# Cosine attention and a cosine-gated MLP on one core: quad 5's softmax sums inverted through DRAM instead of spread by TensorE

## The chip, the cores and the metric

One Trainium2 chip, one of its cores. The metric is the time of one execution on the device in microseconds (us); the kernel before has a median of 417.52 us in three runs (416.75 to 418.28).

## What is computed

The reference is attention with normalised queries and keys, followed by a two-layer network whose activation is h cos(h):

```python
q_n = q / (norm(q, axis=-1) + 1e-06)            # q, k, v: 8 batches x 12 heads x 448 x 64
k_n = k / (norm(k, axis=-1) + 1e-06)
attn = softmax(q_n @ k_n.T / tau)               # tau = 0.1
x = (attn @ v), heads side by side              # 3584 tokens x 768
h = x @ w_in                                    # 768 x 2048
out = (h * cos(h)) @ w_out                      # 2048 x 768
```

## The kernel before, in words

**Quads and blocks.** Four heads of one batch make a *quad*; a batch has 3 quads, so there are 24, and quad n belongs to block n // 3 (a block is one batch of 448 tokens). For each quad the squares of its queries and keys are formed (L491, on POOL), summed (L495, DVE), turned into inverse norms (L521 and L524 on ACT, L527 and L530 on DVE), and the scaled copies Qn and Kn are made (L542, POOL). A transposing DMA (L585, issued by SP) turns them into qT and kT; quads 3 and 4 are transposed on TensorE (L564).

**Scores.** A quad has 7 score steps. A step is four 64x64 matmuls (L601) into a pair of PSUM banks, and one exp on ACT (L608) that writes the bf16 tile E. Three bank pairs take turns. When the 7 steps are done, an AV product of 28 matmuls (`gather`, L637) sums E with V, and DVE copies it to AVs (L644).

**Dividing by the sums.** The softmax is divided late. For a *round* of one or two quads, `sums` (its matmuls are L724) adds E over the keys by a matmul with a 0/1 matrix, with 32-column tiles, so that a row of sums stands in 16 equal partitions. ACT takes the log and the exp of its negative (L733, L734), which is the inverse. This has to be multiplied to AVs, where a sum's value is needed in 64 partitions. So SP writes the rows to a DRAM scratch `rscr` (L737) and reads them back, each row into 64 partitions, into the tile R (L743, two reads for a quad, 224 KB each); then POOL multiplies AVs by R into xT (L748, one instruction for both column blocks of a quad). There are two R tiles: quad n uses R[n % 2]. The rounds are [3, 4], [5], [6, 7], [8, 9] and so on; quads 0 to 2 are done otherwise.

**Quad 5 alone** is treated differently in the kernel before. It is the last quad of block 1 and its inverse is needed first of all by the second W1 stage. Its inverse is written to a corner of gT (`Zg`) that is still free, two matmuls in float32 with a selecting matrix `selB` spread it over the partitions in PSUM (`spread_out`, L759; each is two instructions in the trace), and DVE multiplies AVs with that bank (L761), a column block at a time. `selB` is made by an iota on POOL (L395) and a compare on DVE (L397) at the start.

**The MLP.** Block c's W1 stage is 96 matmuls (L774, 128x448), in 8 pairs of 6-step sums over xT's six column blocks (two for each quad). Each pair goes through ACT, DVE, ACT, DVE (L792, L793, L795, L798) into gT. The first `early` pairs of a stage are started with the blocks 0 to 3 only, as one instruction group that waits for all four, and are completed later with blocks 4 and 5: for block 0 two pairs, for the others one. Between the W1 stages, the W2 matmuls of the block (L833, 128x384, 16 to a sum) are dealt out between the scores of coming quads; DVE copies their sums to osb (L851) and SP stores them (L857).

**What sets the order.** The program is first written as a list of operations with an engine, a reading and a writing set; each engine then works strictly in order. For the head and for the stage from the first W1 to the second (operations 0 to 538), the order on all engines is written out by hand as permutations (HEAD and STAGE). From there on TensorE keeps the program's order and a planner orders ACT, DVE, POOL and SP by a cost and due time of each operation; LEADS moves the due time of some of them. Waits between engines follow from what each operation reads and writes.

The spread's call, which the change removes, is this, in `sums`:

```python
if alone:
    return [lambda bk, a=a: spread_out(quads[0], a, bk) for a in range(2)]
```

Of the kernel before, what the change touches and what calls it, by code (L numbers as in the profile page):

```python
# [8 lines left out]
ALU = mybir.AluOpType  # L9
AX = mybir.AxisListType  # L10
F32 = mybir.dt.float32
BF16 = mybir.dt.bfloat16
I32 = mybir.dt.int32
# [7 lines left out]
class Planner:  # L21
# [60 lines left out]
    def flow(self, until):  # L82
# [25 lines left out]
        (1198, 8, -18.7),  # L108
        (555, 8, -10.5),
        (829, 20, -0.8),  # L110
# [194 lines left out]
def bass_cosine_attention__then__act_gcu_kernel(  # L305
# [9 lines left out]
    B, NH, S, D = q.shape  # L315
# [46 lines left out]
    selB = gT.ap().bitcast(F32)[:, NNB - 2:, S // 2:S // 2 + 128]  # L362
    Zg = gT.ap().bitcast(F32)[0:64, NNB - 4:NNB - 2, S // 2:]
    in_g = [("g", 1, NNB - i) for i in range(1, 5)]
# [6 lines left out]
    def bank(i, n=S, p0=0, p1=128):  # L371
        return PS.ap()[p0:p1, 512 * i:512 * i + n]
# [11 lines left out]
    def fill_sel(e):  # L384
# [9 lines left out]

    op("pool", 0.5, lambda e: e.iota(selB.bitcast(I32), [[-16, 2], [-32, 2], [0, 64]], base=0, channel_multiplier=1),  # L395
       w=["selB"] + in_g)
    op("dve", 0.3, lambda e: e.tensor_scalar(selB, selB.bitcast(I32), 0, None, ALU.is_equal), r=["selB"],  # L397
       w=["selB"] + in_g)
# [29 lines left out]
    def whole(bk):  # L428
        return cut("B", bk, ALL[0])
# [281 lines left out]
    def sums(quads, bk):  # L711
# [3 lines left out]
        alone = quads == [2 * QB - 1]  # L715
        z = int(alone)
# [13 lines left out]
        zz, src, at = Zs[0].ap()[0:32 * np_, :], bank(bk, S, 0, 32 * np_), [("Zs", z)]  # L730
        if alone:
            zz, src, at = Zg, src.rearrange("p (c f) -> p c f", c=2), at + in_g
        act("exp", 0.43, lambda e: e.activation(zz, src, ACT.Ln, bias=0.0, scale=1.0), r=whole(bk), w=at, lead=LEAD)  # L733
        act("exp", 0.45, lambda e: e.activation(zz, zz, ACT.Exp, bias=0.0, scale=-1.0), r=at, w=at, lead=LEAD)  # L734
        if alone:
            return [lambda bk, a=a: spread_out(quads[0], a, bk) for a in range(2)]
        op("sp", 0.6, lambda e: e.dma_start(rscr.ap()[8 * n:8 * n + rows, :], Zs[0].ap()[0:32 * np_:16, :]),  # L737
           r=[("Zs", z)], w=[("rs", n)], dma=("rs", z), moves=0.05, lead=LEAD)
        for i, qd in enumerate(quads):
# [7 lines left out]
            def product(qd=qd, u=u, sl=sl, b=b, c0=c0):  # L747
                op("pool", 2.04, lambda e: e.tensor_tensor(  # L748
                    xT[b % 2].ap()[:, c0:c0 + 2, :], AVs[sl].ap(), R[u].ap(), ALU.mult),
                    r=[("AV", sl), ("R", u, 0), ("R", u, 1)], w=[("x", b % 2, c0), ("x", b % 2, c0 + 1)], lead=LEAD)  # L750
# [5 lines left out]

    def spread_out(qd, a, bk):
        sl, b, c0 = qd % NA, qd // QB, 2 * (qd % QB)
        op("pe", 0.95, lambda e: e.matmul(bank(bk), selB[0:64, a, :], Zg, start=True, stop=True),  # L759
           r=[("Zs", 1), "selB", *in_g], w=whole(bk), mode="b")  # L760
        op("dve", 0.57, lambda e: e.tensor_tensor(xT[b % 2].ap()[:, c0 + a, :], AVs[sl].ap()[:, a, :], bank(bk), ALU.mult),  # L761
           r=[("AV", sl)] + whole(bk), w=[("x", b % 2, c0 + a)], lead=LEAD)
# [154 lines left out]
    def warm(n, bk=0):  # L917
# [35 lines left out]
    )  # L953
    HEAD = (
# [307 lines left out]
```

## Time and profile before

| | |
|---|---|
| median of three runs | 417.52 us (416.75 to 418.28) |
| the profiled execution, its own time | 417.49 us |
| its span, first to last instruction | 415.7 us |
| TensorE clock granted | 1.0 throughout |
| second W1 stage begins (chain) | 89.08 us |

The page's times are microseconds from the span's start. PE is TensorE, DVE VectorE, ACT ScalarE, POOL GpSimd, SP the engine that only issues DMAs. "Chain that ended last" is the sequence of pieces, followed back from the last instruction, each of which released the next. In the lists, "out<-in" are the kernel's tile names, and a bracket behind a row gives the idle time ahead of it and what ended it. Matmuls overlap and their ends are modelled, so a group's length is best read from the starts in the chain. Between the profiled execution's time and its span lie 1.8 us.

### The profile page before, as it was taken

The page shows a single profiled execution, that of the slowest core. Times are in us where ns is not written, and L with a number is a line of the kernel's source. Part 1 is how long each engine was busy: PE and PEld are TensorE (multiplying, and loading weights), DVE is VectorE, ACT ScalarE, POOL GpSimd, SP SyncE. Part 2 cuts the span into 40 slices and gives each one's busy share as a digit, 9 for nine tenths or more (in the row PEclk, how much of TensorE's full clock was granted, in tenths as well). Part 3 has the DMA queues.
Part 4 walks back from the last instruction along what each step waited for, and adds up shares of the span by engine and source line. Part 5 has one row for each costly group of instructions (what it writes and reads, how often), then busy time and mean ns, then how long its engine had stood idle before and what let it go on. Part 6 is the DMA issues. An engine that isn't in the chain of part 4 may idle for free.

```text
span 415.7 us, 8622 instructions
## 1 busy us (share of the span) xinstructions
PE 408.1 (98%) x3629; PEld 216.6 (52%) x3629; DVE 265.2 (64%) x359; ACT 304.8 (73%) x422; POOL 209.4 (50%) x145
## 2 busy tenths in 40 slices
PE   7999999999999999999999999999999999999996
PEld 6455545445554545545554555554554555555565
DVE  5887986567956559655985539845882328736931
ACT  5999899978988678886886757987797656605700
POOL 2666957898299971787429852477403214000000
PEclk9999999999999999999999999999999999999999
DMA  8999997957999996299518993099203423031023
GB/s 267 255 249 205 270 204 150 205 140 134 256 259 240 215 220 169 61 215 255 140 30 167 186 328 89 21 226 170 80 2 82 131 75 91 1 77 38 2 74 78
DMA packets 67224, 62.97 MB, mean 151 GB/s; under 512 B 36385, under 2 KB 59633, under 8 KB 67185
## 3 DMA queue, kind: packets, MB, share of 16 engines
q1 hardware_dynamic: 54816, 50.57, 48.2%
q0 software_dynamic: 12288, 11.80, 18.7%
q8 instruction: 28, 0.46, 0.5%
q14 instruction: 12, 0.09, 0.1%
q10 hardware_dynamic: 80, 0.05, 0.0%
HBM read 54.79 MB, written 11.15 MB: 159 GB/s over the span
## 4 chain that ended last, share of the span: by engine, by line
PE 91%; ACT 4%; DVE 3%; DMA 1%; issue 0%; SPq 0%; ACTq 0%
PE PS L774 35%; PE PS L833 34%; PE PS L601 8%; PE PS L637 7%; PE PS L724 4%; ACT E L608 2%; DMA Kf<-in_k_dram 1%; PE PS L667 1%; PE PS L810 1%; PE PS L618 1%; DVE Qn L542 1%; PE PS L564 1%; DVE n L495 0%; PE PS L759 0%; ACT ar L795 0%; ACT ar L792 0%
## 5 line engine op out<-in xcount | busy, mean ns | idle before, releaser
L608 ACT ACTIVATE E<-PS 128x896 bf16<-128x896 f32 x168 | 143.8, 922 | 19.4 <-PE PS L601 18.0
L833 PE MATMUL PS<-W,gT 128*128 128x384 bf16 x880 | 153.4, 327 | 0.0
L774 PE MATMUL PS<-xT,W 128*128 128x448 bf16 x768 | 147.8, 353 | 0.1
L833 PEld LDWEIGHTS PS<-W,gT 128*128 128x128 bf16 x880 | 81.8, 98 | 68.5 <-issue 14.8
L774 PEld LDWEIGHTS PS<-xT,W 128*128 128x128 bf16 x768 | 74.3, 98 | 71.0 <-issue 1.5
L792 ACT ACTIVATE ar<-PS 128x896 int32<-128x896 f32 (+1 forms) x72 | 59.0, 829 | 47.7 <-PE PS L774 47.1
L793 DVE SCALAR_TENSOR_TENSOR ar<-ar,PS 128x896 f32<-128x896 int32 (+1 forms) x72 | 69.3, 979 | 32.8 <-ACT ar L792 32.7
L748 POOL TENSOR_TENSOR xT<-AVs,R 128x896 bf16<-128x896 f32 x20 | 41.6, 2089 | 61.3 <-DMA R<-rscr 61.3
L798 DVE TENSOR_TENSOR gT<-PS,ar 128x896 bf16<-128x896 f32 (+1 forms) x72 | 69.3, 983 | 3.1 <-ACT ar L795 2.8
L795 ACT ACTIVATE ar<-ar 128x896 f32<-128x896 f32 (+1 forms) x72 | 60.7, 861 | 7.7 <-DVE ar L793 6.9
L851 DVE COPY osb<-PS 128x384 f32<-128x384 f32 x54 | 30.0, 556 | 53.7 <-PE PS L833 53.0
L542 POOL TENSOR_TENSOR Qn<-Qf,rr 128x896 bf16<-128x896 f32 x21 | 35.4, 1686 | 38.4 <-DVE rr L530 38.2
L601 PE MATMUL PS<-qT,kT 64*64 64x448 bf16 x672 | 49.0, 359 | 1.8 <-DVE kT L575 0.8
L644 DVE COPY AVs<-PS 128x896 f32<-128x896 f32 x21 | 22.9, 1090 | 31.3 <-PE PS L637 31.3
L491 POOL TENSOR_TENSOR sqk<-Kf 128x896 bf16<-128x896 f32 x21 | 35.3, 1680 | 13.3 <-DMA Kf<-in_k_dram 7.2
L491 POOL TENSOR_TENSOR sqq<-Qf 128x896 bf16<-128x896 f32 x21 | 35.3, 1682 | 8.9 <-DVE n L495 4.6
L542 POOL TENSOR_TENSOR Kn<-Kf,rr 128x896 bf16<-128x896 f32 (+1 forms) x22 | 36.6, 1668 | 0.0
L637 PE MATMUL PS<-E,Vb 64*64 64x448 bf16 x588 | 31.4, 349 | 0.0
L601 PEld LDWEIGHTS PS<-qT,kT 64*64 64x64 bf16 x672 | 15.3, 105 | 27.0 <-issue 9.8
L495 DVE TENSOR_REDUCE n<-sqk 128x14 f32<-128x896 bf16 (+2 forms) x24 | 24.9, 1039 | 3.6 <-POOL sqk L491 2.9
L495 DVE TENSOR_REDUCE n<-sqq 128x14 f32<-128x896 bf16 (+2 forms) x24 | 24.8, 1037 | 2.2 <-POOL sqq L491 2.1
L451 POOL DMA_DIRECT2D Vb<-in_v_dram x24 | 18.0, 750 | 16.4 <-PE PS L601 9.7
(68 smaller groups left out, 200.8 us busy)
## 6 DMA issues: line engine op xcount, KB each, us to landing
Qf<-in_q_dram SPq DMA_DIRECT2D x24, 448.0 KB, 5.0
out_dram<-osb SPq DMA_DIRECT2D x54, 192.0 KB, 3.0
Kf<-in_k_dram SPq DMA_DIRECT2D x23, 448.0 KB, 5.9
R<-rscr SPq DMA_DIRECT2D x40, 224.0 KB, 4.4
Vb<-in_v_dram POOLq DMA_DIRECT2D x24, 224.0 KB, 7.9
W<-in_moe_w_in_dram POOLq DMA_DIRECT2D x4, 768.0 KB, 11.3
W<-in_moe_w_out_dram POOLq DMA_DIRECT2D x4, 768.0 KB, 11.7
Kf<-in_k_dram SPq DMA_DIRECT2D x1, 320.0 KB, 4.7
```

The lines of the kernel that those rows point to most:

```text
L491: op(eng, (1.64 if eng == "pool" else 1.05) * n, lambda e: e.tensor_tensor(dst, src, src, ALU.mult), r=cut(nm + "f", s, part), w=at, after ...
L495: return op("dve", 0.05 + 0.94 * n, lambda e: e.tensor_reduce(out=n2[u].ap()[:, H * w:H * w + H] if part == ALL[0] else jr(n2[u], w, part) ...
L542: lambda e: e.tensor_tensor(n[u].ap()[:, j0:j1].rearrange("p j r d -> p r j d"), f[s].ap()[:, :, j0:j1], rb, ALU.mult),
L601: ins = e.matmul(bank(bs + r, S, 64 * a, 64 * a + 64), kT[u].ap()[64 * r:64 * r + 64, j, a, :], qT[u].ap()[64 * r:64 * r + 64, :, a, :], s ...
L608: act("exp", 0.806, lambda e: e.activation(E[es].ap(), two(bs), ACT.Exp, bias=0.0, scale=INV_TAU), r=pair(bs), w=[("E", es)], chain="E")
L637: ins = e.matmul(bank(bs + a, S, 64 * r, 64 * r + 64), Vb[vs].ap()[64 * a:64 * a + 64, r, j, :], E[es[j]].ap()[64 * a:64 * a + 64, r, :], ...
L774: ins = e.matmul(bank(bk + i2), W1.ap()[:, i, 128 * nb:128 * nb + 128], xT[c % 2].ap()[:, i, :], start=(i == 0), stop=(i == NKC - 1))
L792: op("act", 0.055 + 0.375 * n, lambda e: e.activation(ai, src, ACT.Identity, bias=0.25, scale=INV2PI), r=bs, w=at)
L793: op("dve", 0.06 + 0.47 * n, lambda e: e.scalar_tensor_tensor(a, ai, -2.0 * math.pi, src, ALU.mult, ALU.add), r=bs + at, w=at)
L795: act("sin", 0.09 + 0.375 * n, lambda e: e.activation(a, a, ACT.Sin, bias=GUARD * math.pi / 2.0, scale=GUARD), r=at, w=at)
L798: op("dve", 0.07 + 0.47 * n, lambda e: e.tensor_tensor(gT.ap()[:, f0:f1, col:col + S], src, a, ALU.mult), r=bs + at, w=[("g", c % 2, f) fo ...
L833: ins = e.matmul(bank(bk, HW), gT.ap()[:, f, col:col + 128], W2.ap()[:, f, HW * h:HW * h + HW], start=(f == 0), stop=(f == NNB - 1))
```

## The change

Quad 5's round goes the way of the other rounds: its inverse is written to DRAM and read back into R[1]. Its multiplication by AVs is done by DVE in two instructions, one for each column block, where the other quads have one on POOL. The two spreading products, their two DVE multiplications, `selB`, `Zg` and the two operations that made `selB` are gone. Block 1's W1 stage now starts two pairs early, as block 0's, instead of one. HEAD is the same order with the two removed operations left out; STAGE is another order; LEADS has one entry instead of three.

```diff
     LEADS = (
-        (1198, 8, -18.7),
-        (555, 8, -10.5),
-        (829, 20, -0.8),
+        (844, 1, -0.4),
     )
...
-    op("pool", 0.5, lambda e: e.iota(selB.bitcast(I32), [[-16, 2], [-32, 2], [0, 64]], base=0, channel_multiplier=1),
-       w=["selB"] + in_g)
-    op("dve", 0.3, lambda e: e.tensor_scalar(selB, selB.bitcast(I32), 0, None, ALU.is_equal), r=["selB"],
-       w=["selB"] + in_g)
...
-        zz, src, at = Zs[0].ap()[0:32 * np_, :], bank(bk, S, 0, 32 * np_), [("Zs", z)]
-        if alone:
-            zz, src, at = Zg, src.rearrange("p (c f) -> p c f", c=2), at + in_g
+        zz, src, at = Zs[0].ap()[0:32 * np_, :], bank(bk, S, 0, 32 * np_), ["Zs"]
...
-        if alone:
-            return [lambda bk, a=a: spread_out(quads[0], a, bk) for a in range(2)]
...
             def product(qd=qd, u=u, sl=sl, b=b, c0=c0):
+                if qd == 2 * QB - 1:
+                    for a in range(2):
+                        op("dve", 0.54, lambda e, a=a: e.tensor_tensor(
+                            xT[b % 2].ap()[:, c0 + a, :], AVs[sl].ap()[:, a], R[u].ap()[:, a], ALU.mult),
+                            r=[("AV", sl), ("R", u, 0), ("R", u, 1)], w=[("x", b % 2, c0 + a)], lead=LEAD)
+                    return
...
-    def spread_out(qd, a, bk):
-        sl, b, c0 = qd % NA, qd // QB, 2 * (qd % QB)
-        op("pe", 0.95, lambda e: e.matmul(bank(bk), selB[0:64, a, :], Zg, start=True, stop=True),
-           r=[("Zs", 1), "selB", *in_g], w=whole(bk), mode="b")
-        op("dve", 0.57, lambda e: e.tensor_tensor(xT[b % 2].ap()[:, c0 + a, :], AVs[sl].ap()[:, a, :], bank(bk), ALU.mult),
-           r=[("AV", sl)] + whole(bk), w=[("x", b % 2, c0 + a)], lead=LEAD)
...
-        late, early = 2 * (QB - 1), 1 if c else 2
+        late, early = 2 * (QB - 1), 1 if c > 1 else 2
```

STAGE's numbers say little to a reader, so here are the two orders resolved into instructions where they differ around the change.

PE, from the AV product of quad 3 (63.85 in the trace before) to the second W1 stage. V is an AV product, S a score step (S2: two of them), Mn a run of n W2 matmuls, T a transpose of seven 128x128 blocks, Z the sums of a round, P a spreading product; a bar is a change between groups of different tile shape (T and M have the same).

```
before  V S | M2 T T | S2 | M7 | S3 | Z(3,4) | V S2 | M6 | S2 | M8 | S2 V S | Z(5) | S3 | M14
        | S3 | M6 | P | S2 V S | P | S2 | M5, W1
after   V S | M4 T | S | T | S | M4 | S2 | Z(3,4) | S V S | M1 | S | M4 | S2 | M6 | S | M1
        | S V S2 | Z(5) | S3 | M14 | S2 | M9 | S2 V S | M5 | S2 | W1
```

SP, from the load of quad 9's query on (Q and K are loads of a query or key tile into the slot named, qT and kT transposing DMAs, "write" and "read" those of the scratch):

```
before  Q[0], K[0], qT(7), write(3,4), kT(7), read x2 R[1], read x2 R[0], Q[1], K[1], qT(8), kT(8), Q[2], stores ...
after   Q[0], write(3,4), K[0], qT(7), Q[1], kT(7), read x2 R[1], read x2 R[0], write(5), K[1], qT(8), kT(8),
        read x2 R[1] for quad 5, store, store, store, Q[2], stores ...
```

POOL, from quad 7's query scaling on:

```
before  Qn(7), square K, Kn(7), square Q, square K, square Q, product(3), product(4), square Q, Qn(8), square K, ...
after   Qn(7), square K, Kn(7), square Q, square K, Qn(8), Kn(8), product(3), product(4), square Q, square K, V load, ...
```

DVE, the last operations of the stage: before, AVs copy of quad 6, norm steps and the second multiplication of quad 5, norm steps, an osb copy, two norm sums (L495); after, AVs copy, a norm step, two osb copies, a norm step, a norm sum, the two multiplications of quad 5, a norm sum. On ACT the logs and exps (L733, L734) of rounds [3, 4] and [5] stand closer together than before: one score's exp lies between the two of [3, 4] (before four), none between the two of [5] (before three).

More of the change, by code (lines that the diff above doesn't have):

```diff
@@ L361, in bass_cosine_attention__then__act_gcu_kernel @@
     ident = sb("ident", [128, 128], BF16)
-    selB = gT.ap().bitcast(F32)[:, NNB - 2:, S // 2:S // 2 + 128]
-    Zg = gT.ap().bitcast(F32)[0:64, NNB - 4:NNB - 2, S // 2:]
-    in_g = [("g", 1, NNB - i) for i in range(1, 5)]
     sel = sb("sel", [128, 32], BF16)
@@ L714, in sums @@
         summed.update(quads)
-        alone = quads == [2 * QB - 1]
-        z = int(alone)
         np_ = 2 * len(quads)
@@ L729, in sums @@
            mode="s")
-        zz, src, at = Zs[0].ap()[0:32 * np_, :], bank(bk, S, 0, 32 * np_), [("Zs", z)]
-        if alone:
-            zz, src, at = Zg, src.rearrange("p (c f) -> p c f", c=2), at + in_g
+        zz, src, at = Zs[0].ap()[0:32 * np_, :], bank(bk, S, 0, 32 * np_), ["Zs"]
         act("exp", 0.43, lambda e: e.activation(zz, src, ACT.Ln, bias=0.0, scale=1.0), r=whole(bk), w=at, lead=LEAD)
         act("exp", 0.45, lambda e: e.activation(zz, zz, ACT.Exp, bias=0.0, scale=-1.0), r=at, w=at, lead=LEAD)
-        if alone:
-            return [lambda bk, a=a: spread_out(quads[0], a, bk) for a in range(2)]
         op("sp", 0.6, lambda e: e.dma_start(rscr.ap()[8 * n:8 * n + rows, :], Zs[0].ap()[0:32 * np_:16, :]),
-           r=[("Zs", z)], w=[("rs", n)], dma=("rs", z), moves=0.05, lead=LEAD)
+           r=["Zs"], w=[("rs", n)], dma=("rs", 0), moves=0.05, lead=LEAD)
         for i, qd in enumerate(quads):
```

56 rows, old and new, of tables (HEAD, STAGE) are left out of this document.

## The prediction

> **What bounds the kernel now.** I read the page first: its line of engines and the chain that ended last.
>
> ```profile
> span 415.7 us, 8622 instructions
> PE 408.1 (98%) x3629; PEld 216.6 (52%) x3629; DVE 265.2 (64%) x359; ACT 304.8 (73%) x422; POOL 209.4 (50%) x145
> PE 91%; ACT 4%; DVE 3%; DMA 1%; issue 0%; SPq 0%; ACTq 0%
> ```
>
> TensorE is the bound nearly everywhere: a microsecond that leaves its queue is gained, and one in which it waits is lost. Then the busy time by stretches, around the place of the change (columns: stretch, its length, busy us and instructions of PE, PEld, DVE, ACT, POOL, then clock, DMA share, GB/s).
>
> ```profile
> 77.00:78.00 1.00, 1.00 (x20) 0.44 (x14) 0.67 (x1) 1.00 (x2) 1.00 (x1) 1.00 0.51 113
> 79.00:80.00 1.00, 1.00 (x15) 0.43 (x8) 0.42 (x1) 1.00 (x2) 1.00 (x2) 1.00 0.05 5
> 81.00:82.00 1.00, 1.00 (x10) 0.49 (x12) 0.49 (x1) 1.00 (x3) 0.47 (x1) 1.00 0.91 262
> ```
>
> PE is full there at full clock (1.00 behind POOL's column), ACT nearly, and the DMA has holes at 77 to 80. Last, the chain in order of time (start, us, what):
>
> ```profile
> 58.50 0.94 ACT E L608
> ...
> 63.85 1.42 PE PS L637 x28
> ...
> 77.47 1.43 PE PS L724 x14
> 78.90 0.69 PE PS L601 x12
> 79.59 2.38 PE PS L833 x14
> ...
> 83.75 0.95 PE PS L759 x2
> 84.69 0.50 PE PS L601 x8
> 85.20 1.32 PE PS L637 x28
> 86.71 0.95 PE PS L759 x2
> 87.66 0.50 PE PS L601 x8
> 88.16 0.92 PE PS L833 x5
> 89.08 2.27 PE PS L774 x12
> ...
> 339.74 18.16 PE PS L774 x96
> 357.90 15.60 PE PS L833 x96
> ```
>
> Until 63.85 an exp (L608) still appears on the chain; from there to the second W1 stage (L774, from 89.08) every piece is PE's. One W1 matmul costs 18.16/96 = 0.189, one W2 matmul 15.60/96 = 0.1625. The chain also prices a change between groups of unlike tile shape: eight L601 matmuls take 0.50 and twelve 0.69, so four cost 0.19 and 0.12 is fixed; fourteen W2 matmuls take 2.38 for 14 x 0.1625 = 2.28, fixed 0.10. I use 0.115 for a **switch**.
>
> **PE's part of the change.** The two spreading products (L759) go: 0.95 each with the switch into it, 1.90 together. But the new written order cuts PE's work into smaller groups. By the two resolved lists shown with the diff, from quad 3's AV product (63.85) to the second W1 stage, the old one has 20 switches, 2 of them inside the two 0.95; the new one has 25. That adds (25 - 18) x 0.115 = 0.80. Scores, AV products, sums, transposes and W2 matmuls are the same in number. So PE could start W1 1.90 - 0.80 = 1.10 earlier, at 87.98. Ahead of 63.85 the new list has four more switches too (15 for 11); there an exp sets the pace, so I take 0, with 0.46 as the upper bound and 0.3 of gain as the lower, since one score is issued earlier.
>
> Another engine limits that start. W1's early parts wait for all four blocks of quads 3 and 4 at once, and POOL writes them (L748).
>
> ```profile
> 74.86 1.69 POOL L542 TENSOR_TENSOR Kn<-Kf,rr 128x896 bf16<-128x896 f32 x1
> 76.51 1.68 POOL L491 TENSOR_TENSOR sqq<-Qf 128x896 bf16<-128x896 f32 x1
> 78.15 1.68 POOL L491 TENSOR_TENSOR sqk<-Kf 128x896 bf16<-128x896 f32 x1
> 79.79 1.68 POOL L491 TENSOR_TENSOR sqq<-Qf 128x896 bf16<-128x896 f32 x1
> 83.77 4.12 POOL L748 TENSOR_TENSOR xT<-AVs,R 128x896 bf16<-128x896 f32 x2 [2.30 <-DMA R<-rscr]
> 87.85 1.68 POOL L491 TENSOR_TENSOR sqq<-Qf 128x896 bf16<-128x896 f32 x1
> ```
>
> POOL now idles 2.30 for R. The new list puts four operations of about 1.65 between the key scaling that ends at 76.55 and the products, where three stood: free at 76.55 + 4 x 1.65 = 83.15, still ahead of R. So the products stay at 83.77 and end at 83.77 + 4.12 = 87.89. PE and POOL thus both allow W1 at 88.0, no earlier, and **1.1 us is the most the change can give**.
>
> **Quad 5's inverse by the DRAM trip.** What was PE work becomes a chain through SP, the DMA, POOL's release of a buffer and DVE. SP's issues, before:
>
> ```profile
> 76.91 1.24 SPq L585 DMA_TRANSPOSE kT<-Kn  x1
> 78.19 3.53 SPq L743 DMA_DIRECT2D R<-rscr  x4
> ...
> 94.01 0.61 SPq L737 DMA_DIRECT2D rscr<-Zs  x1
> ...
> 325.16 2.51 SPq L743 DMA_DIRECT2D R<-rscr  x4
> ```
>
> The sum of quad 5 (L724) ends in the new order one stretch ahead of W1: three scores 0.69, fourteen W2 2.38, two scores 0.50, nine W2 9 x 0.1625 + 0.115 = 1.58, three scores with an AV product 86.71 - 84.69 = 2.02, five W2 0.92, two scores 0.50, a switch 0.115: 8.7 before 88.0, at 79.3. In the next round the sum ends at 92.78 (rows below) and SP issues the write at 94.01, 1.2 later.
>
> ```profile
> 91.35 1.44 PE PS L724 x28
> ```
>
> So the write could go at 80.5. SP is in order, and the four reads of R for quads 3 and 4 hold it until 78.19 + 3.53 = 81.7; the write goes then, behind it a K load and quad 8's two transposing DMAs, which wait for POOL's scalings of quad 8 (done by 83.15) and take some 1.25 each. None of this decides: the read of quad 5's R fills R[1], which the first of the two products (quad 3's) reads until 83.77 + 2.06 = 85.83. **That release is the gate.** The two reads go at 85.9 and 86.5 (0.6 each). From the second read's issue to the reader's start it was 83.77 - 78.79 = 5.0 behind a transposing transfer, and in a quiet queue, by the row below, 329.84 - 325.76 = 4.1.
>
> ```profile
> 329.84 4.11 POOL L748 TENSOR_TENSOR xT<-AVs,R 128x896 bf16<-128x896 f32 x2 [13.32 <-DMA R<-rscr]
> ```
>
> The new place has a transposing transfer ahead of it, but one issued a little longer before: I take 4.6, so 91.1. DVE then makes the two products. Nothing shows this form at 448 columns, but at 896 columns with both inputs in SBUF:
>
> ```profile
> 32.50 1.09 DVE L691 TENSOR_TENSOR xT<-AVs,ar 128x896 bf16<-128x896 f32 x1 [0.46 <-ACT ar L682]
> ```
>
> 1.1 for both halves: 92.2, and 0.1 for the signal: PE may go on at 92.3. On DVE the norm sum (L495) of a query load is ahead of them; its POOL square ends at 87.89 + 1.65 = 89.5, so it is done by 90.7.
>
> **Two pairs early.** With one pair PE would have 8 matmuls to do without quad 5, now 16: 16 x 0.189 = 3.02. It stands still from 88.0 + 3.02 = 91.0 until 92.3, for 1.3. Before, the same sixteen matmuls would have been done at 89.08 + 3.02 = 92.1. The balance is 92.3 - 92.1 = **+0.2**: the 1.1 of PE time is given back at the wait, and a little more.
>
> **SP's new order.** One load of 448 KB (the query of the slot that quad 7 leaves) was issued at 81.77, behind the reads of R, and now goes ahead of quad 7's key transpose and these reads. At 262 GB/s (row 81:82) it needs 448/262 = 1.7. The DMA's holes at 77:78 (0.49) and 79:80 (0.95) can take 1.44 of it; I take the rest, +0.3, between 0 and 1.7. Whatever it costs moves the products, R[1]'s release and W1 alike.
>
> **What is hidden.** The constants at the head that go (an iota, a compare) ran while DVE waited for its first data:
>
> ```profile
> 4.73 0.43 DVE L491 TENSOR_TENSOR sqk<-Kf 128x256 bf16<-128x256 f32 x1 [2.58 <-DMA Kf<-in_k_dram]
> ```
>
> 0, and no loss either. The exps, logs and norms stay in number. LEADS only ranks ACT, DVE, POOL and SP after the first 538 operations; PE's list there stays as it was, and as the last W1 and W2 stages on the chain run without a piece of another engine between them, these orders can gain little or nothing; a loss is possible, 0 to 1; I take 0.
>
> **Sum.** -1.90 + 0.80 + 1.30 + 0.3 = +0.5. The profiled execution took 417.49, its span 415.7; the median of the three is 417.52, so the sum may stand against either: **418.0**.
>
> **Rivals.**
>
> *The trip is in time.* If R's reads land as in the quiet queue (4.1) and quads 3 and 4 come some 0.8 earlier, the wait vanishes: 417.49 - 1.1 = 416.4. For it: POOL's fourth operation leaves 0.6 of room, and quads 3 and 4's log and exp are now next to each other, so their write leaves earlier. Against it: those reads stand behind quad 7's key transpose in SP, whose key POOL delivers no earlier.
>
> *The load ahead of the reads is not absorbed* (the other side: slower). If the holes at 77:80 come from the transposing transfer itself, during which nothing behind it moves, the 448 KB add to the line in full: 1.7 instead of 0.3, 419.4. It decides from the point where R of quad 3 lands later than 83.8. For it: at 79:80 four reads were pending and 5 GB/s moved. Against it: the load is issued some 1.5 ahead of the transpose.
>
> *DVE's products wait for POOL.* Both inputs are now in SBUF, and POOL has arithmetic again from 87.85 on, in operations of 1.68. If one shuts the other out, a product waits for up to a whole POOL operation: 418.0 + 1.7 = 419.7. The trace has no such pair side by side: at 32.50, the one late DVE product with two SBUF inputs, POOL had no arithmetic. [...] What speaks against a full loss: behind two squares, at about 87.89 + 2 x 1.65 = 91.2, the new list has POOL issue a V load, with no arithmetic.
>
> *The orders do something else.* A wait in the first W1 stage (transposes moved, scalings later on POOL) or after the second: up to +2, or a gain of some tenths.
>
> **How the numbers follow.** Forecast 0.45, trip in time 0.17, load not absorbed 0.15, products blocked 0.16, other orders 0.07. The measurement cannot tell less than 0.3% (1.25 us) from no change: within is 416.3 to 418.8. The forecast lies within save for 0.06 of it that falls above; the first rival puts 0.10 below and 0.07 within, since its 416.4 is at the edge; the next two put 0.28 above and 0.03 within; the last 0.04 below and 0.03 above or so. Faster 0.14, same 0.49, slower 0.37. The range runs from the first rival's edge, 416.2, to a blocked product with a slow landing, 420.2; the far ends of rivals one to four, some 0.17, stay outside.
>
> **What would show it.** No L759 rows; W1's second stage starts near 88.0 to 88.4 in a first piece of 16 matmuls, then PE idles 1 to 2 us, released by DVE's new product. Quad 3's product starts at 83.8 to 84.2; the two late reads of R are issued just after it ends; DVE's products start 4.1 to 5.0 after the second. If the first product starts by 83.0 or there is no idle time after the sixteenth matmul, the first rival is right; if the first product starts at 85 or later, the second; if R has landed and DVE's product still starts late, at the end of a POOL operation, the third. If PE loses time outside 50 to 95, I have the wrong place.

## The result, and the profile after

The changed kernel takes 427.14 us (median of five runs, 426.42 to 430.18) against 416.75 (416.73 to 418.28) for the kernel before on the same chip: ratio 1.0244, 95% interval 1.0224 to 1.0264. The forecast was 418.0 and its range ended at 420.2; the true loss is 10.4 us. The profiled execution took 427.26 us. The ratios below leave out the runs that lie over 1.5% above the fastest of their kernel, three of them far outside all others (598.87, 839.07 and 2356.62 us).

The page of the kernel after: its span, its engines, and the shares of the chain that ended last.

```profile
span 425.5 us, 8620 instructions
...
PE 409.0 (96%) x3625; PEld 215.1 (51%) x3625; DVE 271.0 (64%) x358; ACT 304.6 (72%) x422; POOL 209.1 (49%) x144
...
PE 82%; DVE 5%; ACT 4%; POOL 4%; DMA 3%; issue 1%; SPq 0%; POOLq 0%
```

PE's busy time hardly changed, from 408.1 to 409.0 us. But its share of the chain fell from 91% to 82%: other engines stand on it. Line numbers are those of each kernel; in the kernel after POOL's product is L738, the reads of R L727, the transposing DMA L575, DVE's product L734, W1 L757, the sums L712 and W2 L816. The chain in order of time (start, us, what), from the product that frees R[1] to the second W2 stage:

```profile
85.07 2.09 POOL xT L738
87.16 0.24 SPq L575
...
87.50 0.54 SPq L727
...
88.07 3.81 DMA R<-rscr
...
91.93 7.50 DVE xT L734 x2
...
99.48 1.67 PE PS L757 x4
101.16 2.73 PE PS L712 x17
...
118.68 3.90 PE PS L816 x24
```

W2 begins at 118.68 instead of 108.89, 9.79 later. From there to the end both kernels take the same 306.8 us (425.5 - 118.68, 415.7 - 108.89). So the whole loss lies in one stage, and it has three parts. The timeline of all engines there (start, us, engine, line, operation; in brackets the idle time ahead and its releaser) shows the largest:

```profile
89.33 3.19 PE L757 MATMUL PS<-xT,W 128*128 128x448 bf16 x16 [0.95 <-POOL xT L738]
...
90.79 1.68 POOL L481 TENSOR_TENSOR sqk<-Kf 128x896 bf16<-128x896 f32 x1
...
91.93 7.49 DVE L734 TENSOR_TENSOR xT<-AVs,R 128x448 bf16<-128x448 f32 x2
92.41 0.76 POOL L441 DMA_DIRECT2D Vb<-in_v_dram  x1
...
93.19 1.70 POOL L532 TENSOR_TENSOR Qn<-Qf,rr 128x896 bf16<-128x896 f32 x1
...
94.83 0.76 POOL L441 DMA_DIRECT2D Vb<-in_v_dram  x1
...
95.61 1.70 POOL L532 TENSOR_TENSOR Kn<-Kf,rr 128x896 bf16<-128x896 f32 x1
97.26 1.68 POOL L481 TENSOR_TENSOR sqq<-Qf 128x896 bf16<-128x896 f32 x1
...
99.48 0.93 PE L757 MATMUL PS<-xT,W 128*128 128x448 bf16 x2 [6.96 <-DVE xT L734]
```

The two products of DVE fill 7.49 us. The view of their line splits that (shortest, median and longest in ns, first and last start):

```profile
L734 DVE TENSOR_TENSOR xT<-AVs,R x2: 1016/3786/6556, 91.9 to 92.9; 128x448 bf16<-128x448 f32 x2
```

The first took 1.016 and the second 6.556 us for the same work. The second ends at 99.48, half a microsecond after POOL's square (97.26 + 1.68 = 98.94): it went through only when POOL stopped computing. Note where the wait is written: not as idle time of DVE but inside its instruction's duration. The stretches of the window view (length; busy us and instructions of PE, PEld, DVE, ACT, POOL; then granted clock, DMA share, GB/s) show what PE's standing still did in turn:

```profile
94.00:98.00 4.00, 0.00 (x0) 0.00 (x0) 4.00 (x1) 0.00 (x0) 3.98 (x4) 0.91 1.03 243
98.00:102.00 4.00, 2.52 (x16) 0.88 (x20) 2.43 (x2) 0.81 (x1) 3.75 (x4) 0.50 1.28 216
102.00:106.00 4.00, 4.00 (x35) 1.58 (x24) 1.15 (x2) 2.11 (x5) 0.27 (x1) 0.74 1.23 260
```

PE had no matmul from 92.5 (89.33 + 3.19) on. A mean of 0.91 in 94:98 (1.00 in 96:97, 0.64 in 97:98, 0.50 in 98:99) means half clock for the last 0.7 us, so the clock fell at 97.3; 0.74 in 102:106 means that it came back at 104.1, when PE had been working for 4.6 us. The sum, against the profile before: W1 starts at 89.33 instead of 89.08, **+0.25**; its sixteen matmuls (3.02 at 0.189 each) are done at 89.33 + 3.02 = 92.35 and PE goes on at 99.48, **+7.13**; from there to W2 it takes 118.68 - 99.48 = 19.20 where the same 80 matmuls and sums took 108.89 - 89.08 - 3.02 = 16.79, **+2.41**. Together 9.79.

### The profile page after: what moved, and what is told of

Same layout as the page of the kernel before. It is cut to its first block, busy times and chain, and to the rows that moved or that the text cites. A ratio compares the mean times of both kernels' runs of the same rounds, so it can differ in the third digit from the quotient of the medians.

```text
span 425.5 us, 8620 instructions
## 1 busy us (share of the span) xinstructions
PE 409.0 (96%) x3625; PEld 215.1 (51%) x3625; DVE 271.0 (64%) x358; ACT 304.6 (72%) x422; POOL 209.1 (49%) x144
## 4 chain that ended last, share of the span: by engine, by line
PE 82%; DVE 5%; ACT 4%; POOL 4%; DMA 3%; issue 1%; SPq 0%; POOLq 0%
PE PS L757 33%; PE PS L816 31%; PE PS L591 7%; PE PS L627 5%; PE PS L712 3%; DMA R<-rscr 2%; ACT E L598 2%; DVE xT L734 2%; POOL Qn L532 1%; DVE n L485 1%; DMA Kf<-in_k_dram 1%; POOL sqq L481 1%; POOL Kn L532 1%; POOL sqk L481 1%; ACT ar L778 1%
## 5 line engine op out<-in xcount | busy, mean ns | idle before, releaser
L757 PE MATMUL PS<-xT,W 128*128 128x448 bf16 x768 | 148.9, 354 | 7.9 <-DVE xT L734 7.0
L816 PE MATMUL PS<-W,gT 128*128 128x384 bf16 x880 | 154.2, 327 | 0.0
L816 PEld LDWEIGHTS PS<-W,gT 128*128 128x128 bf16 x880 | 81.4, 98 | 69.3 <-issue 15.7
L757 PEld LDWEIGHTS PS<-xT,W 128*128 128x128 bf16 x768 | 74.1, 98 | 80.0 <-DVE xT L734 7.4
L738 POOL TENSOR_TENSOR xT<-AVs,R 128x896 bf16<-128x896 f32 x20 | 41.6, 2088 | 72.8 <-DMA R<-rscr 72.5
L591 PE MATMUL PS<-qT,kT 64*64 64x448 bf16 x672 | 50.1, 360 | 2.8 <-ACT E L598 1.4
```

The costliest lines, as they stand in the source:

```text
L591: ins = e.matmul(bank(bs + r, S, 64 * a, 64 * a + 64), kT[u].ap()[64 * r:64 * r + 64, j, a, :], qT[u].ap()[64 * r:64 * r + 64, :, a, :], s ...
L757: ins = e.matmul(bank(bk + i2), W1.ap()[:, i, 128 * nb:128 * nb + 128], xT[c % 2].ap()[:, i, :], start=(i == 0), stop=(i == NKC - 1))
L816: ins = e.matmul(bank(bk, HW), gT.ap()[:, f, col:col + 128], W2.ap()[:, f, HW * h:HW * h + HW], start=(f == 0), stop=(f == NNB - 1))
```

## The experiments

The theory: POOL's arithmetic shuts out DVE's product, whose two inputs both lie in SBUF. Its rivals: the V loads that POOL issues shut it out; or the cause is outside POOL (the copies of R, the memory). In the expectations P is the first, D the second, M the third. In the first four kernels the orders behind operation 538 were planned anew, with side effects of their own; in all later ones every order but the named moves is that of the kernel after.

**POOL held back.** The next V load on POOL, and all behind it, waits until DVE's second product (`x5`; `x4` is the first) is done:

```diff
+moved([(("pool", ("V", 3)), ("dve", ("x", 1, 5)))], [(("pool", ("V", 3)), ("dve", ("x", 1, 5)))])   # pool_waits
...
+v = find("pool", ("V", 3))               # pool_waits_only, the run after it
+v.deps.append(x5.i)
```

> POOL's queue from the V load behind the second square on waits until DVE has made quad 5's second product; nothing else is edited. Theory P (POOL arithmetic shuts DVE's two-SBUF products out): both products are done within 1.6 us of their start at about 91.9, PE goes on at about 93.3, waits about 0.9 instead of 7.0, the clock stays at 1.0 and the time falls by some 8.5 to 418.5. [...] Theory M (DVE is slowed by the DMA traffic or by R itself, POOL has no part): the second product stays at 6 us or more and the time at 427.

422.27 us, ratio 1.0111 (1.0075 to 1.0146): the two products took 1.55 us from 91.64, and PE waited 1.0 for them. Some 2 us of the rest is a side effect: in the third W1 stage PE waited 4.1 us for a product of POOL. The same wait with the later orders kept:

> As pool_waits, but with the order of every engine kept exactly as in the changed kernel to its end, so that no later stage moves: the one difference is that POOL's V load behind the second square, and so all behind it, waits for DVE's second product. Theory P: products done by 93.4, PE waits 1.0, clock 1.0, time 418.8 to 419.3 (6.0 of the wait and the 2.4 at the lower clock go from 427.1); the further 3 of pool_waits, a wait for POOL in the third W1 stage, is not there. Theory M: 427.

419.78 us, 1.0057 (1.0039 to 1.0076). Nothing was taken from the transfers or the computation, only POOL's place in time, and of the 10.4 us above the kernel before 2.4 are left (its 417.36 on that chip).

**What of POOL it is.** First the two V loads moved behind the key scaling, so that POOL's arithmetic runs without a break; then the reverse, four V loads beside the products and the arithmetic behind them. POOL's order in words, before on the left:

```diff
-V load, Qn, V load, Kn            +Qn, Kn, V load, V load                (v_loads_later)
-V load, Qn, V load, Kn, ...       +4 V loads, Qn (waits for x5), Kn, ... (v_loads_only)
```

> The two V loads that POOL issues between the scalings of quad 9 go behind them, so that while DVE makes quad 5's products POOL has arithmetic alone, without a gap. Theory P: the second product still waits for the whole run of arithmetic, about 92.5 to 97.5, and takes 4 us or more; time 425 to 427. Theory D: it takes 0.6, PE goes on near 93.4, time 418.5. Theory M: unchanged, 427.

> All four V loads stand together behind the second square and the scalings of quad 9 wait for DVE's second product, so that POOL only issues loads while DVE multiplies. Theory P: the products take at most 1.6 together, PE goes on near 93.4, time 418.5. Theory D: the second product waits for the loads, three of 0.75, ends near 95.5, time about 421. Theory M: unchanged, 427.

425.04 us, 1.0155 (1.0119 to 1.0192), and 419.69 us, 1.0040 (1.0024 to 1.0056). The timelines, arithmetic alone first, V loads alone second:

```profile
93.06 3.04 DVE L734 TENSOR_TENSOR xT<-AVs,R 128x448 bf16<-128x448 f32 x2
93.54 2.08 POOL L532 TENSOR_TENSOR Qn<-Qf,rr 128x896 bf16<-128x896 f32 x1
...
95.59 2.06 POOL L532 TENSOR_TENSOR Kn<-Kf,rr 128x896 bf16<-128x896 f32 x1
...
96.16 1.60 PE L757 MATMUL PS<-xT,W 128*128 128x448 bf16 x4 [2.51 <-DVE xT L734]
```

```profile
91.06 1.68 POOL L481 TENSOR_TENSOR sqk<-Kf 128x896 bf16<-128x896 f32 x1
...
92.22 1.55 DVE L734 TENSOR_TENSOR xT<-AVs,R 128x448 bf16<-128x448 f32 x2
...
92.69 2.91 POOL L441 DMA_DIRECT2D Vb<-in_v_dram  x4
```

Beside four V loads the products are not held up: they take 1.55, of which 0.5 is the end of the square. So D falls as a cause by itself. Beside arithmetic, each product got its turn at the end of one operation of POOL (1.015 and 2.103 us), and that operation's successor was stretched from 1.70 to 2.08 and 2.06: here the one waited for the other, in both directions. P had expected 4 us or more here, and the two took 3.04: arithmetic without a break does not shut DVE out for its whole run. So either the V loads between the scalings or the moment at which the products came has a part in the 6.56; these runs do not tell which. The time fell little all the same, because W1 started 1.1 later (90.47) and the wait of 2.51 was followed by matmuls at half clock (1.60 for four and 2.44 for the sums, where v_loads_only needed 0.93 and 1.47; with the 1.67 that four took at 0.50 in the kernel after, I estimate a clock of 0.50 from 96.3 to 99.7).

**One input out of SBUF.** ACT copies R into a free PSUM bank pair, and DVE's products read it there:

```diff
+op("act", 0.86, lambda e: e.activation(two(2), R[u].ap(), ACT.Identity), ...)
-xT[b % 2].ap()[:, c0 + a, :], AVs[sl].ap()[:, a], R[u].ap()[:, a], ALU.mult)
+xT[b % 2].ap()[:, c0 + a, :], AVs[sl].ap()[:, a], two(2)[:, a], ALU.mult)
```

> ACT, idle there, copies R into a free pair of PSUM banks, and DVE multiplies AVs in SBUF with that: one SBUF input for each product; POOL's queue is as in the changed kernel. Theory P: the copy takes 0.92, each product 0.62 beside POOL's arithmetic, PE goes on at about 94.1 and waits 1.7, clock 1.0, time about 419.3. [...] Theory M: the copy out of R is slow in place of the product, 425 or more.

422.22 us, 1.0115 (1.0084 to 1.0147), with 1.7 us lost in a later stage to the new plan. At the place itself:

```profile
91.62 0.92 ACT L734 ACTIVATE PS<-R 128x896 f32<-128x896 f32 x1 [1.53 <-DMA R<-rscr]
...
92.58 1.15 DVE L737 TENSOR_TENSOR xT<-AVs,PS 128x448 bf16<-128x448 f32 x2 [0.74 <-ACT PS L734]
93.01 1.71 POOL L532 TENSOR_TENSOR Qn<-Qf,rr 128x896 bf16<-128x896 f32 x1
```

The second product runs beside the very scaling that shut it out before, and is no longer for it (1.15 for the two). ACT's reading of R, with the same transfers beside it, takes 0.92, as its exps of that size do. So neither the memory nor the transfers are slow, and M falls.

**One product instead of two,** 896 columns wide:

```diff
+P.both = lambda e: e.tensor_tensor(xT[1].ap()[:, 4:6, :], AVs[1].ap(), R[1].ap(), ALU.mult)
...
+x4.fn = self.both
+seq["dve"].remove(x5)
```

> DVE makes quad 5's product in one instruction of 896 columns in place of two of 448; all orders kept, POOL unhindered. Theory P, with DVE getting its turn when the POOL operation in progress ends: the product starts in the second square, gets in at its end near 92.4, is done at 93.5; PE goes on at 93.6, time about 419. Theory P2 (DVE gets no turn at all as long as POOL has arithmetic queued): it ends near 99.5 to 100, time 427.

419.53 us, 1.0050 (1.0031 to 1.0069).

```profile
91.03 1.68 POOL L525 TENSOR_TENSOR sqk<-Kf 128x896 bf16<-128x896 f32 x1
...
92.18 1.48 DVE L1254 TENSOR_TENSOR xT<-AVs,R 128x896 bf16<-128x896 f32 x1
...
93.43 1.77 POOL L576 TENSOR_TENSOR Qn<-Qf,rr 128x896 bf16<-128x896 f32 x1
```

It waits for the square's end (92.7) and is done at 93.66. So DVE got a turn when this operation of POOL ended; the second, separate product needed a second turn and did not get it. Of 10.4 us above the kernel before 2.2 are left: four fifths of the damage hung on that split.

**The clock by itself.** 112 small matmuls on a constant, into a bank that is written anew afterwards, fill PE's wait; their output is not used, and nothing else is changed:

```diff
+new(early, self.dummy, [o.i for o in exps], after=early)   # 112 matmuls of 128x128x128
```

> 112 matmuls of 128x128 on a free bank, of no use to the result, stand in PE's queue between the early parts of the second W1 stage and their completion, some 6.3 us, so that PE is not idle in the wait; all else as in the changed kernel. If the granted clock of 0.5 behind the wait comes from PE's idleness: the clock stays at 1.0, PE still goes on at about 99.5, and the time falls by 2.4 to 424.7. If it comes from something else (DMA, DVE): the clock falls as before and the time stays at 427.

425.59 us, 1.0197 (1.0178 to 1.0216); DVE's products still take 7.50. The clock is 1.00 in and behind the wait, and there PE needs 0.93 and 1.47 us for the four matmuls and the sums, where the kernel after needed 1.67 and 2.73: 2.0 less. The time is 8.2 above the kernel before on its chip (417.36), where the kernel after is 10.4 above. So some 2 us are the clock, and the idle PE is its cause.

**The query load** back behind quads 3 and 4's reads of R:

```diff
+put(find("sp", ("Qf", 1, 0)), find("sp", ("rs", 1)))
```

> In SP's queue the load of the query that the change had moved ahead of quad 7's key transpose goes back behind the four reads of R and the write for quad 5; all else as in the changed kernel. If the load's 448 KB stood in the reads' way: quad 3's product starts at 83.8 instead of 85.1, W1 at 88.2 instead of 89.3, quad 5's R lands 1.2 earlier. The time falls by 1.1 at least, to 426; by up to 9, if the two products then fall beside POOL's V load and not its scalings. If the load was not in the way: 85.1 and 427 again.

425.00 us, 1.0188 (1.0160 to 1.0216).

```profile
82.85 4.15 POOL L777 TENSOR_TENSOR xT<-AVs,R 128x896 bf16<-128x896 f32 x2
83.90 3.13 SPq L614 DMA_TRANSPOSE kT<-Kn  x1
...
87.12 1.18 SPq L766 DMA_DIRECT2D R<-rscr  x2
...
87.47 3.20 PE L796 MATMUL PS<-xT,W 128*128 128x448 bf16 x16
...
91.00 1.70 POOL L571 TENSOR_TENSOR Qn<-Qf,rr 128x896 bf16<-128x896 f32 x1
92.46 3.67 DVE L773 TENSOR_TENSOR xT<-AVs,R 128x448 bf16<-128x448 f32 x2 [2.63 <-DMA R<-rscr]
92.63 0.76 POOL L480 DMA_DIRECT2D Vb<-in_v_dram  x1
...
93.41 1.70 POOL L571 TENSOR_TENSOR Kn<-Kf,rr 128x896 bf16<-128x896 f32 x1
```

Quad 3's product starts 2.2 earlier than after (82.85 for 85.07), right behind POOL's scalings, and W1 at 87.47. So the load did cost what it weighs. But quad 5's R comes no earlier (92.46, after 91.93): R[1] is free at 84.9, and the reads go out at 87.12, when the issue of quad 8's key transpose lets SP go. That is a **second gate**. In the kernel after it ended at 87.40 (87.16 + 0.24 in the chain), just behind R[1]'s release at 87.16.

**Past the second gate.** One product, the load behind, and the two reads ahead of that transpose; then the same with a third early pair, and with one early pair instead of two:

```diff
+put(kt, find("sp", ("R", 1, 1)))                     # early_reads: kt is quad 8's key transpose
+at = new(o, ... f(e, nb, i2, 0, 4), ..., after=at)   # third_pair: pair 2's blocks 0 to 3 behind pair 1's
+put(second[0], at); put(second[1], second[0])        # one_early_pair: pair 1's first part behind the sums
```

> One product of 896 columns instead of two, the query load behind quads 3 and 4's reads of R, and quad 5's two reads issued ahead of quad 8's key transpose; all other orders as in the kernel after. With the load behind, quad 3's product started at 82.85 and ended at 84.93, but the reads were issued only at 87.12, when the key transpose's issue (3.13 us, from 83.90) let SP go. If that issue is the second gate: reads at 85.0, R landed at 90.2 to 90.5, product done at 91.9, W1 starts at 87.5, waits 1.2 to 1.5 and goes on at 91.9, some 0.2 ahead of the kernel before: 417.0 to 417.6. Rival (R's arrival is bound by the DMA queue, not by SP's place): R at 92.4, PE waits 3.4 to 3.6, 419.3 or more. If POOL still shuts DVE's product out: POOL's second square ends at 90.2, a V load follows, so at most 0.3 is lost.

> As early_reads, and a third W1 pair started with blocks 0 to 3: 24 matmuls (4.5 us) ahead of quad 5 instead of 16. If the trip is what PE waits for: PE works from 87.5 to 92.0 and the wait is gone, so the stage runs 1.4 to 1.6 ahead of the kernel before: 415.8 to 416.4, faster than both kernels. If R lands at 92.4 all the same (the rival): a wait of 2.0, 419.3. If the bank releases behind it (ACT and DVE work through the pairs) become the bound: the gain stops at 0.5 to 1.0, near 416.8.

> As early_reads, with one W1 pair started early instead of two (the second pair's first part moved behind the sums): 8 matmuls (1.5 us) ahead of quad 5. If the end of the trip sets when PE goes on, all eight matmuls taken away come back as wait: early_reads plus 1.5, near 418.8, with a wait of 2.7 to 3.0. Rival (PE's order ahead of the wait does not matter since ACT and DVE bound the stage): no change against early_reads.

The ratios are 1.0024 (1.0009 to 1.0039), 1.0043 (1.0015 to 1.0070) and 1.0061 (1.0038 to 1.0085), but they leave out slower runs that belong to these kernels: over all runs the medians are 422.30, 420.41 and 424.39 us. early_reads and third_pair fall short of what was expected, and the times of each kernel fell into groups: early_reads six at 417.7 to 420.3 and five at 424.3 to 425.3, third_pair from 417.74 to 425.66, one_early_pair three at 418.9 to 421.5 and three at 427.3 to 427.8. Two profiles, one of 418.88 us (one_early_pair) and one of 424.77 (third_pair), suggest what divides them:

```profile
89.07 1.67 POOL L534 TENSOR_TENSOR sqk<-Kf 128x896 bf16<-128x896 f32 x1
...
90.49 1.20 DVE L1263 TENSOR_TENSOR xT<-AVs,R 128x896 bf16<-128x896 f32 x1 [0.20 <-DMA R<-rscr]
...
91.47 1.77 POOL L585 TENSOR_TENSOR Qn<-Qf,rr 128x896 bf16<-128x896 f32 x1
...
91.75 0.93 PE L810 MATMUL PS<-xT,W 128*128 128x448 bf16 x4 [2.46 <-DVE xT L1263]
```

```profile
91.70 1.70 POOL L588 TENSOR_TENSOR Qn<-Qf,rr 128x896 bf16<-128x896 f32 x1
92.15 4.63 DVE L1266 TENSOR_TENSOR xT<-AVs,R 128x896 bf16<-128x896 f32 x1 [1.62 <-DMA R<-rscr]
...
93.34 0.76 POOL L497 DMA_DIRECT2D Vb<-in_v_dram  x1
...
94.12 1.70 POOL L588 TENSOR_TENSOR Kn<-Kf,rr 128x896 bf16<-128x896 f32 x1
```

R landed at 90.5 in the one and at 92.1 in the other. The first product came ahead of POOL's scaling and took 1.20; the second came 0.45 behind its start and waited through it and the next, for 4.63. The reads do go out early (85.15 and 85.50), so the second gate was real, but R was not there before POOL's scaling in both. That the same divides the runs of one kernel is an inference from these two kernels; third_pair_pool_waits below supports it.

**The product on POOL,** behind its second square, with all other orders as after:

> The kernel after with quad 5's two products on POOL, right behind its second square, instead of on DVE; all other orders as after. If POOL's arithmetic shutting DVE out is the cause: POOL makes the two products from 92.4 in 2 x 1.05 to 94.6 without anything in their way, PE waits 2.0 to 2.4 instead of 7.0 and the clock stays up: 419.8 to 420.5. Rival (R or the memory itself is slow to be read while the queues write beside it): the second product takes several us on POOL too, 423 or more.

421.20 us, 1.0084 (1.0065 to 1.0103). POOL made both from 92.13 in 2.22 us, PE waited 2.17 and the clock stayed at 1.00 in the profile (420.21 us); two other runs, of 421.82 and 421.96, had a mean clock of 0.996. No product was slow here, where the two engines do not compete.

**Kept clear by order.** POOL waits for the one product, with two and with three early pairs; and the product on POOL with three:

```diff
+v.deps.append(x4.i)          # third_pair_pool_waits, early_reads_pool_waits
+put(x4, at, "pool")          # third_pair_on_pool, product_on_pool (there x5 too): at is the second square
```

> As third_pair, and POOL's next V load and with it its scalings wait until DVE's product is done. If POOL's arithmetic in the product's way makes the slower group, it is gone: the product takes 1.0 to 1.5 us in every run, PE waits less than 0.5 behind its 24 matmuls, all runs within 1 us, 416.0 to 417.5. If the bank releases bound the faster group, a wait for DVE or ACT of about 1 us stands in the W1 stage behind the sums, and the time stays near 417.7. Rival (the two groups have another cause, such as the landing of R): both groups stay.

> As early_reads (two early pairs), and POOL waits for DVE's product in the same way. If the theory holds: one group only, 417.0 to 418.0, PE waits 1.0 to 1.5 behind its 16 matmuls. Rival: two groups as before, 418 and 424.5.

> As third_pair, with the one product of 896 columns on POOL right behind its second square instead of on DVE. POOL has no one to wait for but R: product from 90.9 to 93.0, PE waits 1.0 behind its 24 matmuls, one group only, 416.8 to 417.8. Rival (R lands after 92 in some runs): the product ends at 94 and more, 418 to 419, and POOL's later work moves with it.

419.33 us, 1.0038 (1.0013 to 1.0063); 421.37 us, 1.0059 (1.0028 to 1.0090); 419.10 us, 1.0024 (1.0002 to 1.0046). All three fall short of what was expected. With three pairs none of twelve runs lies above 423.1 any more, and with the product on POOL eleven of twelve lie within 418.7 to 420.2. early_reads_pool_waits still has two groups (417.8 to 418.6 and 421.4 to 423.1); its profile, of 422.35 us, loses the difference elsewhere, in waits of 1.6, 1.1 and 1.4 us between 127 and 151. The chain of third_pair_pool_waits shows why no gain came:

```profile
87.89 5.40 PE PS L815 x28
93.29 1.47 PE PS L770 x28
...
94.78 0.55 ACT Zs L777
...
95.36 0.58 ACT Zs L778
...
96.76 1.29 ACT L460
...
99.11 1.10 DVE gT L839
...
100.26 9.25 PE PS L815 x48
```

W1 starts 1.2 ahead of the kernel before and runs through 28 matmuls without a wait for quad 5. Then PE waits 1.65 for a PSUM bank: the next round's log and exp, and the loading of the sine table (1.29), stand on ACT ahead of the pair that holds it.

**That wait moved too.** The sums of quads 6 and 7 go ahead of the third early pair, the table loading right behind their exp, and pair 1 is finished ahead of pair 0:

```diff
+put(z, pe[pe.index(self.ops[541])])      # z: the sums, behind the second early pair
+put(self.ops[555], self.ops[546])        # the table behind the exp
...
+put(p1[0], pe[pe.index(p0[0]) - 1])      # pair 1 ahead of pair 0, on ACT and DVE too
```

> As third_pair_pool_waits, with the sums of quads 6 and 7 behind the second early pair, the sine table loaded right behind their exp, and pair 1 finished ahead of pair 0 on PE, ACT and DVE. If ACT's chain in front of the bank is what PE waits for: Z ends at 92.4, the table stands at 94.9, pair 1's bank is free at 98.8 instead of 100.2 and PE wants it at 98.4, a wait of 0.4 instead of 1.65: 1.2 less than third_pair_pool_waits, 416.5 to 417.8, level with the kernel before or some tenths ahead. Rival (another bank or ACT's throughput bounds): the wait stays over 1 us, 418.0 to 419.

> As third_pair_on_pool, with the same three moves. PE is busy until 93.9 or 94.3 with early pairs and sums, the product on POOL ends at 93.2, so neither wait is left but 0.4 at the bank: 1.5 less than third_pair_on_pool, 417.2 to 417.9. Rival (the bank wait stays): 418.3 or more.

417.88 us, 1.0021 (0.9997 to 1.0046), and 417.76 us, 1.0015 (0.9997 to 1.0033). PE's wait for the bank is 0.56 in both, and the profiled spans are 415.6 and 416.3, as before's 415.7. With all these repairs the change is level with the kernel before, and no version beat both.

## Why the prediction was wrong, point by point

**The step that failed** is DVE's products: "1.1 for both halves: 92.2". They took 7.50. The row behind the 1.1 was of a moment in which POOL had no arithmetic, as the third rival said itself. That rival named the cause, but its price was wrong: one operation of POOL, 1.7. In its place the runs showed three operations and the hand-overs between them (6.56), and the clock behind them. What spoke against a full loss there, a V load of POOL with no arithmetic, did come, at 92.41; but the first product only ended at 92.95, and 0.24 later the scaling began. How long a product is held differs with the turn it gets: 1.015 and 2.103 for products that got theirs at the next end (v_loads_later), 6.556 for one that was passed over twice. The old product, with one input in PSUM, was not held beside POOL's arithmetic: in the trace before it took 0.62 at 84.73 and 0.61 at 87.70 (L761), while POOL's products ran from 83.77 to 87.89 and a square from 87.85. The 0.1 for the signal, which the prediction takes without a row, was 0.05 in the chain after (from 99.43 to 99.48).

**No step had the clock.** All waits were added at their length. The waits of 7.0 (after), 5.5 (q_load_behind) and 4.6 (third_pair) brought PE back at half clock: the next four W1 matmuls took 1.67, 1.68 and 1.67, where they took 0.93 in v_loads_only. That made 2.4 us more in the kernel after. A wait of 2.51 (v_loads_later) did so too, with 1.60 for the four, while one of 2.46 did not (one_early_pair, 0.93). The stretches at 0.50 lasted 6.8 us in the kernel after (97.3 to 104.1) and in third_pair (0.73 in 94:96, 0.50 in 96:100, 0.56 in 100:102), and 3.4 in v_loads_later (the estimate above, 96.3 to 99.7) and, behind its wait of 4.1, in pool_waits (0.83 in 150:160): once or twice 3.4. The cost is half of the part in which PE works: 4.6 / 2 = 2.3 in the kernel after. From the (modelled) end of the last matmul to the clock's fall it was 4.8 us in the kernel after, 2.7 in third_pair and 2.6 in v_loads_later, where PE was at work again when it fell. What decides whether a wait of some 2.5 us costs the clock, these runs do not show.

**SP's query load** was taken at +0.3, between 0 and 1.7. Quad 3's product started at 85.07, against 83.77 before and 82.85 with the load moved back. Over the profiles it started at 84.77 to 86.18 in the eight kernels with the load in front, and at 82.85 to 84.22 in the eight with it behind, 1.75 between the medians. So the second rival held as well, and decided by its own mark ("at 85 or later"): the load cost its full 1.7.

**The release of R[1]** was one of two gates. In the kernel after the product ended at 87.16, and the issue of quad 8's key transpose held SP until 87.40; the reads went at 87.50. "None of this decides" overlooked that transpose, taken at 1.25 and in fact an issue of 3.1 to 4.1 us: it would have held the reads until 87 in any case. From the second read's issue to the product it took 3.8, less than the 4.6 taken.

**PE's part** was right: -1.10 forecast, and from quad 3's AV product to W1's first row PE took 24.12 us in q_load_behind (63.35 to 87.47) and in sums_ahead (63.44 to 87.56) against 25.16 before (63.75 to 88.91), -1.04. Another 0.3 to 0.4 was gained ahead of it. In the kernel after it was never paid out, because POOL's product came late.

**Two pairs early** was right in kind: sixteen matmuls stood before the wait. One_early_pair's lower group has a median of 420.05, early_reads' one of 418.6: 1.45 for the eight matmuls that the second pair put there, whose length is 8 x 0.189 = 1.51. That the size fits so well may be luck: the group of one_early_pair is three runs, 2.6 us apart, two of them with a mean clock of 0.996.

**What was hidden** was hidden: nothing changed behind W2's start (306.8 us in both), so LEADS cost nothing. Neither did the head: quad 3's AV product starts at 63.15 in the timeline after and at 63.75 before.

The range failed because rivals two and three were priced each against the forecast, as if one excluded the other. They came together, 1.3 late and then shut out. But 418.0 + 1.4 + 1.7 = 421.1 would not have reached 427.1 either: the third had no price for being passed over, and no rival had the clock.

**Open** is what decides whether DVE gets its turn at the end of an operation of POOL. It did at the end of a square ahead of a V load (after, one_product, one_early_pair) and between two scalings without a V load (v_loads_later). It did not at the end of a query scaling with a V load behind it, four times out of four (after, matmuls_in_wait, q_load_behind, third_pair), though POOL then computed nothing for 0.72 us, nor at the end of a key scaling with a square right behind it (after, matmuls_in_wait). That a V load between two scalings matters is only an inference from these places.

## What to carry to other kernels

Moving one input of a vector product from PSUM to SBUF can make it compete with what POOL computes at that moment: here a product with both inputs in SBUF took 6.56 us, and two with one input in PSUM took 1.15 together at the same place (r_through_psum). The price is not always one POOL operation: it was three here, and a gap of 0.72 us between two of them did not help. So look at POOL's next seven microseconds, not at its next instruction. If such a product stands on the critical path, make it one instruction, and keep POOL off by order or put the product on POOL itself; a good landing time is not enough when the landing moves by 1.6 us, as between the two profiles above. Before a wait is added to a sum at its length, ask whether TensorE may lose its clock in it: here a wait of 2.51 us did, one of 2.46 did not, and behind the wait of 7.0 the clock cost some 2 us more.

## What the runs showed of the hardware that was not expected

- A DVE product of 0.5 us with both inputs in SBUF (1.09 for both halves in one, while POOL waits, in sums_ahead) took 6.56 us beside two scalings and a square of POOL, and both products together, with one input in PSUM, took 1.15, the second beside the same query scaling (r_through_psum).
- The loser can be POOL too: a scaling of 1.70 took 2.08 when DVE's product got in ahead of it.
- Four V loads issued by POOL in 2.91 us did not hold up DVE's products: 1.55 us for the two, of which 0.5 is the end of a square (v_loads_only).
- The issue of quad 8's key transpose took 3.1 to 4.1 us where it stood within 0.4 us behind the query's, which took 1.24 to 1.64, and it held all of SP's queue. Behind the two reads of R it took 1.29 to 1.30 in one_early_pair and three later kernels, and 2.21 in third_pair.
- TensorE's clock fell to 0.50 between 2.6 and 4.8 us after the last matmul and stayed there for 3.4 or 6.8 us, once behind a wait of only 2.51 us (v_loads_later); 112 matmuls of no use kept it at 1.00.
